# Channel attention folded into a squared-ReLU feed-forward: early weight forms kept in SBUF per batch, late ones loaded singly, sums of squares moved to transfers, rounding of v in the third groups

## The chip, the core and the metric

The program runs on one core of a Trainium2 chip. The metric is the time of one execution on the device in microseconds (us). The kernel before takes 2139.14 us (median of three runs, 2138.82 to 2139.2). Times inside the program come from one profiled execution.

## The reference: what is computed

q, k and v are four batches of 6080 rows and 256 columns, in float32. Each column of q and k is divided by its norm over the 6080 rows; a 256 x 256 matrix of products of k's columns with q's columns is taken over the rows; a softmax over it gives `a`; the rows of v are multiplied by `a` and then go through a feed-forward with 2048 hidden columns.

```python
def _attn_ref(q, k, v, tau):
    qn = q / (np.linalg.norm(q, axis=1, keepdims=True) + 1e-06)
    kn = k / (np.linalg.norm(k, axis=1, keepdims=True) + 1e-06)
    s = kn.transpose(0, 2, 1) @ qn / tau
    s = s - s.max(-1, keepdims=True)
    a = np.exp(s)
    a /= a.sum(-1, keepdims=True) + 1e-09
    return (v @ a).astype(np.float32)

def _moe_ref(x, w_in, w_out):          # x: the 4 x 6080 rows of v @ a
    h = np.maximum(x @ w_in, 0.0)      # w_in 256 x 2048
    return (h * h @ w_out).astype(np.float32)
```

## The kernel before

**The computation as it is arranged.** `a` is multiplied into w_in first: W = a @ w_in (256 x 2048) is made once per batch, and the feed-forward then reads v itself. Float32 precision comes from splitting each operand of a matmul into a high and a low part (`_hi`, `_lo`) and adding three products. A rounding of this kind is two instructions: a cast on ScalarE (ACT) that makes the high part, and a subtraction on VectorE (DVE) that makes the low part.

**Blocks, groups, periods.** In the text the batches are counted 1 to 4; names of tiles carry 0 to 3. The rows of v come in 12 blocks per batch (ten of 512, two of 480). The first two blocks of batch 1 and the last of batch 4 are done plainly. The 45 others are done in four groups of 512 hidden columns each; one group of one block is a period, and the 180 periods are counted by `k` (k = 40, 88 and 136 are the first of batches 2, 3 and 4). A period makes the hidden values by a scheme of seven products of the Strassen kind, in place of eight: seven combinations of quarters of W (the forms A11, S1, S2, A12, S4, S3 and A22) meet seven combinations of quarters of the block of v. TensorE's order in `period(k)` is A11 (into `ps_b`), S1 (`ps_h`), a window of output matmuls of earlier groups, S2 (`ps_c`), A12 (`ps_b`), S4 (`ps_h`), S3 (`ps_c`), matmuls of the attention, another output window, A22 (`ps_c`), another output window. Between them ScalarE and VectorE form sums, ReLU, squares and roundings of the hidden values.

**The attention of the next batch** runs beside these periods: `attention(b)` is a generator that is moved on at fixed points of each period (`side("dve")`, `side("sq")`, `side("pe")`, `side("act")`, `side("mid")`). It takes q and k in 25 chunks, one per period: load, rounding (ACT, DVE), squares (ACT, in place), the product into `gram`, and the addition of the squares into `acc`. After the last chunk come the norms, the softmax, W and the forms of W; these are rounded, stored to DRAM scratch by `keep_blocks` and `keep_sums`, and read back by the periods of the next batch. I call the stretch in which this happens, at the end of each of batches 1 to 3, the forming stretch.

**Forms in the kernel before.** `load_forms(k, late)` brings each period's forms in four transfers: the early forms A11, S1, S2 (two of 384 KB, high and low) and the late ones A12, A22, S3, S4 (two of 512 KB). They lie in the tags `w_hi` and `w_lo` with buffers for two periods; the early ones of period k+2 are asked for after S2 of period k, the late ones of period k+1 after S1 of period k.

**What sets the order.** Each engine runs its instructions in the order in which the program gives them. For SyncE (SP), which issues most loads, the loads of forms and the first chunks of q and k are placed in its queue by the framework's scheduler; the stores of forms and the later chunks stay at their place in the program. An issue whose condition is not met holds back all that stands behind it in SP's queue; the same is true of GpSimd (POOL), which issues the loads of v, the accumulation of partial outputs in DRAM order (`o<-o`), and the outputs.

**v.** `parts_of_v` loads the next block, forms its seven combinations and rounds them in two pieces of 1024 and 768 columns. `v_step` moves it at six points of a block: `V_STEPS` for batches 1 to 3 (both pieces done in the second and third group), `V_LAST` for batch 4 (in the third and fourth).

## Time and profile before

| | us |
|---|---|
| median of three runs | 2139.14 |
| span of the profiled execution | 2137.0 |
| the runs' median less that span | 2.14 |
| TensorE (PE) busy | 2123.9 |
| VectorE busy | 1947.1 |
| ScalarE busy | 1818.6 |
| GpSimd busy | 403.4 |

The profile shows one execution. Its own time is given only as its span, from the first to the last instruction; the runs' median stands 2.14 us above it. The page gives busy time by engine, the chain of work that ended last, and the costliest groups; views of the trace give waits, timelines, and busy time by stretch. A matmul is pipelined with the next, so a busy TensorE is one without a visible hole, not one at its peak. "<-" between tiles means "written from"; "<-" before an engine or a transfer names who ended a wait. All operations are recorded at line 27, the helper that issues them in program order, save the loads that the scheduler places.

### The profile page before, as it was taken

The numbers are of one execution on the slowest core, as the hardware profiler recorded it, in microseconds if no ns is written. First come the engines' busy times: TensorE is split into PE (matmuls) and PEld (weight loads), VectorE is DVE, ScalarE is ACT, GpSimd is POOL, SyncE is SP. The second block draws the span as 40 slices with busy tenths as digits, with TensorE's granted clock in tenths as the row PEclk, the third lists the DMA queues.
The fourth block names the chain that finished last, engine by engine and source line by source line (L and its number), as shares of the span: only waits on it lengthen the run. The fifth ranks groups of instructions, "written<-read, shape, count | busy, mean of one in ns | idle before, by whom it ended". The sixth has DMA issues, their size and how long they took to land.

```text
span 2137.0 us, 43905 instructions
## 1 busy us (share of the span) xinstructions
PE 2123.9 (99%) x16990; PEld 2066.1 (97%) x16990; DVE 1947.1 (91%) x2577; ACT 1818.6 (85%) x2708; POOL 403.4 (19%) x506
## 2 busy tenths in 40 slices
PE   9999999999999999999999999999999999999999
PEld 8789999999999999999999999999999999999998
DVE  6898999998999999988999999999899999999993
ACT  5887888888888888878888888878888999999995
POOL 0000121211222121221222121121212122122121
PEclk9999999999999999999999999999999999999999
DMA  9777888889998888788999788887999788788783
GB/s 345 234 232 264 240 255 252 235 239 283 303 297 262 251 251 262 234 241 247 292 303 288 248 255 257 249 234 229 325 322 314 233 241 252 220 247 248 233 256 86
DMA packets 258865, 548.24 MB, mean 257 GB/s; under 512 B 26848, under 2 KB 120672, under 8 KB 258656
## 3 DMA queue, kind: packets, MB, share of 16 engines
q1 hardware_dynamic: 193696, 449.32, 62.3%
q0 software_dynamic: 64960, 96.11, 20.9%
q8 instruction: 134, 2.20, 0.4%
q14 instruction: 75, 0.61, 0.1%
HBM read 431.75 MB, written 64.23 MB: 232 GB/s over the span
## 4 chain that ended last, share of the span: by engine, by line
PE 89%; DVE 6%; ACT 2%; DMA 2%; issue 1%; SPq 0%; DVEq 0%; ACTq 0%
PE ps_o L27 41%; PE ps_c L27 16%; PE ps_h L27 14%; PE ps_b L27 11%; PE gram L27 4%; DVE x L27 2%; PE ps_w L27 2%; PE ps_o_m L27 1%; ACT x L27 1%; DMA wf<-wf_kept 1%; DVE s_lo L27 1%; DVE acc L27 1%; DMA qk<-in_k 1%; DVE A_lo L27 0%; DMA qk<-in_q 0%
## 5 line engine op out<-in xcount | busy, mean ns | idle before, releaser
L27 DVE TENSOR_TENSOR s_lo<-x,s_hi 128x1024 fp32r<-128x1024 f32 (+1 forms) x384 | 464.0, 1208 | 44.4 <-ACT s_hi L27 44.1
L27 PE MATMUL ps_c<-v_hi,wf 128*128 128x256 f32 (+1 forms) x2160 | 466.9, 280 | 4.4 <-DVE x L27 2.2
L27 POOL DMA_DIRECT2D o<-o x225 | 245.4, 1253 | 1102.7 <-ACT o L27 689.7
L27 ACT CAST s_hi<-x 128x1024 fp32r<-128x1024 f32 (+1 forms) x384 | 399.7, 1041 | 37.6 <-DVE x L27 27.9
L27 DVE TENSOR_TENSOR x<-x 128x1024 f32<-128x1024 f32 (+3 forms) x540 | 389.6, 722 | 10.3
L27 PEld LDWEIGHTS ps_c<-v_hi,wf 128*128 128x128 f32 x2160 | 367.4, 188 | 7.8 <-ACT ps_c L27 3.3
L27 ACT ACTIVATE x<-x 128x512 f32<-128x512 f32 (+2 forms) x540 | 350.0, 648 | 21.7 <-DVE x L27 9.2
L27 PE MATMUL ps_b<-v_hi,wf 128*128 128x256 f32 (+1 forms) x1440 | 309.7, 279 | 1.8 <-DVE nx L27 1.1
L27 PE MATMUL ps_h<-v_hi,wf 128*128 128x256 f32 (+1 forms) x1440 | 309.1, 278 | 0.0
L27 PE MATMUL ps_c<-v_lo,wf 128*128 128x256 f32 (+1 forms) x1080 | 300.9, 279 | 0.0
L27 DVE TENSOR_TENSOR A_lo<-x,A_hi 128x1024 fp32r<-128x1024 f32 (+3 forms) x360 | 276.9, 792 | 18.8 <-ACT A_hi L27 15.3
L27 ACT CAST A_hi<-x 128x1024 fp32r<-128x1024 f32 (+3 forms) x360 | 254.4, 707 | 38.4 <-DVE x L27 25.5
L27 PEld LDWEIGHTS ps_b<-v_hi,wf 128*128 128x128 f32 x1440 | 245.2, 188 | 2.3 <-DVE nx L27 1.3
L27 PEld LDWEIGHTS ps_h<-v_hi,wf 128*128 128x128 f32 x1440 | 244.9, 188 | 0.0
L27 ACT COPY x<-ps_c 128x512 f32<-128x512 f32 (+1 forms) x180 | 105.1, 584 | 158.3 <-PE ps_c L27 158.0
L27 PEld LDWEIGHTS ps_c<-v_lo,wf 128*128 128x128 f32 x1080 | 203.2, 188 | 0.1
L27 PE MATMUL ps_b<-v_lo,wf 128*128 128x256 f32 (+1 forms) x720 | 200.6, 279 | 0.0
L27 PE MATMUL ps_h<-v_lo,wf 128*128 128x256 f32 (+1 forms) x720 | 200.4, 278 | 0.0
L27 DVE TENSOR_TENSOR x<-x,ps_h 128x512 f32<-128x512 f32 (+1 forms) x180 | 122.4, 680 | 76.9 <-PE ps_h L27 76.6
L27 PE MATMUL ps_o<-s_hi,wo_hi 128*128 128x256 f32 (+3 forms) x954 | 190.1, 295 | 0.5 <-ACT s_hi L27 0.5
L27 PE MATMUL ps_o<-s_hi,wo_lo 128*128 128x256 f32 (+3 forms) x954 | 190.2, 295 | 0.0
L27 PE MATMUL ps_o<-s_lo,wo_hi 128*128 128x256 f32 (+3 forms) x954 | 190.0, 295 | 0.1
(166 smaller groups left out, 5166.9 us busy)
## 6 DMA issues: line engine op xcount, KB each, us to landing
wf<-wf_kept SPq DMA_DIRECT2D x360, 512.0 KB, 5.3
wf<-wf_kept SPq DMA_DIRECT2D x360, 384.0 KB, 4.9
o<-o POOLq DMA_DIRECT2D x114, 256.0 KB, 5.9
qk<-in_k SPq DMA_DIRECT2D x87, 256.0 KB, 4.3
qk<-in_q SPq DMA_DIRECT2D x87, 256.0 KB, 4.8
v<-in_vT POOLq DMA_DIRECT2D x76, 256.0 KB, 5.1
out_T<-o POOLq DMA_DIRECT2D x152, 128.0 KB, 4.7
o<-o POOLq DMA_DIRECT2D x76, 128.0 KB, 6.2
```

The costliest lines, as they stand in the source:

```text
L27: return lambda *args, **kwargs: self.tc.keep_in_program_order(issue(*args, **kwargs))
```

## The change

It has three parts.

1. **Forms.** The early forms of a batch and group (768 KB, high and low together) get a buffer of their own for each of the four groups (`w_own0` to `w_own3`, 6 KB per partition) and are loaded once per batch by `load_early`; the other periods of the batch use what is there. The late forms come singly, 256 KB each (high and low of one form), through a ring of four buffers of 2 KB per partition (`w_ring`): `load_late(k + 1, form)` stands right behind the product of period k that used the same form. The scratch in DRAM is cut to match (`wf_early`, `wf_later`), so a part of the form sums is stored in three transfers instead of two. SBUF for forms stays 32 KB per partition. W itself (batch 1, and the last block) uses pieces of the same buffers, and the first chunks of q and k use `w_own` and four tags of the hidden values as landing space.
2. **Squares.** For the attentions of batches 3 and 4 (which run beside batches 2 and 3), the 24 additions on VectorE per batch become accumulating transfers issued by GpSimd, as it already was for five chunks of batch 2. The chunk loaded next is one earlier than before, and the softmax begins one period later, so the forms of batch 3 are stored one period later and those of batch 4 two.
3. **Roundings of v.** `V_LAST` holds for all batches: the pieces of 1024 and 768 columns are rounded in the third group and at the start of the fourth.

```diff
@@ Gram.add_squares
-                if self.b == 1 and c < HEAD:
+                if self.b > 1 or self.b == 1 and c < HEAD:
                     pool_engine.dma_start(a, sq, accum_op=ALU.add)
@@ attention(b)
         def add_and_load(c):
             g.add_squares(c)
+            c -= b > 1
             if c0 <= c and c + ahead < g.n:
                 load(c + ahead)
...
         yield from until("mid")
         add_and_load(g.n - 1)
         yield
+        if b > 1:
+            yield from until("mid")
+            yield
         yield from until("dve")
         yield from softmax_and_W(b)
@@ keep_sums
-        early, later = wf_kept[b, g, i]
         src = part.bitcast(F32).rearrange("p (r s m) -> p r s m", r=2, s=4)
-        issue(early[:, :, 1:3, :], src[:, :, 0:2, :])
-        issue(later[:, :, 2:4, :], src[:, :, 2:4, :])
+        issue(wf_early[b, g][:, i, :, 1:3, :], src[:, :, 0:2, :])
+        for s, form in ((2, S3), (3, S4)):
+            issue(wf_later[b, g, form[0]][:, i], src[:, :, s, :])
@@ forms of a period
-    def load_forms(k, late):
-        if k < len(groups):
-            b, _, j = groups[k]
-            for i in range(2):
-                n = (3, 4)[late]
-                t = WF[k, late, i] = wpool.tile([P, 2, n, P], F32R, tag=("w_hi", "w_lo")[late], name=f"wf{k}_{late}_{i}")
-                nc.sync.dma_start(t.bitcast(F32), wf_kept[b, j, i][late])
...
+    def load_early(k):
+        if k >= len(groups):
+            return
+        b, n, j = groups[k]
+        if k >= GPB and groups[k - GPB][0] == b:
+            WF[k, 0] = WF[k - GPB, 0]
+            return
+        own = own_tile(j, 3 * 2 * 2 * P, F32R, f"wf{k}_own")
+        WF[k, 0] = own.rearrange("p (i r s m) -> p i r s m", i=2, r=2, s=3)
+        nc.sync.dma_start(WF[k, 0].bitcast(F32), wf_early[b, j])
+
+    def load_late(k, form):
+        if k < len(groups):
+            b, n, j = groups[k]
+            f = form[0]
+            t = ring_tile([P, 2, 2, P], f"wf{k}_{f}")
+            WF[k, f] = t.rearrange("p i r (s m) -> p i r s m", s=1)
+            nc.sync.dma_start(t.bitcast(F32), wf_later[b, j, f])
+        elif form in (A12, S4):
+            load_plain((A12, S4).index(form))
@@ v_step
+    V_LAST_FROM = 0
-        steps = V_LAST if b == B - 1 else V_STEPS
+        steps = V_LAST if b >= V_LAST_FROM else V_STEPS
@@ period(k)
         product(k, H, S1, T1, start=True)
-        load_forms(k + 1, 1)
...
-        load_forms(k + 2, 0)
+        load_early(k + 2)
...
         product(k, B2, A12, B21)
+        load_late(k + 1, A12)
...
         product(k, H, S4, B22)
+        load_late(k + 1, S4)
...
         product(k, C, S3, T3)
+        load_late(k + 1, S3)
...
         product(k, C, A22, T4)
+        load_late(k + 1, A22)
```

**SP's queue inside batch 3.** The rows are the loads of forms of periods 92 and 93 (`wf<period>_<piece>`; 128x768 is 384 KB, 128x1024 is 512 KB, 128x512 is 256 KB) and the chunks of q and k (`qk3_..`). Before:

```order
L983 DMA wf92_1_0_14723<-wf_kept2_0_0_4_154 128x1024
L983 DMA wf92_1_1_14725<-wf_kept2_0_1_4_156 128x1024
L420 DMA qk3_4_14670<-in_k 128x512
L421 DMA qk3_4_14670<-in_q 128x512
L983 DMA wf93_0_0_14759<-wf_kept2_1_0_3_157 128x768
L983 DMA wf93_0_1_14761<-wf_kept2_1_1_3_159 128x768
L983 DMA wf93_1_0_14876<-wf_kept2_1_0_4_158 128x1024
L420 DMA qk3_5_14835<-in_k 128x512
L421 DMA qk3_5_14835<-in_q 128x512
L983 DMA wf93_1_1_14878<-wf_kept2_1_1_4_160 128x1024
```

After:

```order
L1013 DMA wf92_3_14825<-wf_later2_0_3_171 128x512
L1013 DMA wf92_4_14883<-wf_later2_0_4_172 128x512
L435 DMA qk3_4_15021<-in_k 128x512
L436 DMA qk3_4_15021<-in_q 128x512
L1013 DMA wf93_1_14947<-wf_later2_1_1_173 128x512
L1013 DMA wf93_2_14959<-wf_later2_1_2_174 128x512
L1013 DMA wf93_3_14969<-wf_later2_1_3_175 128x512
L435 DMA qk3_5_15160<-in_k 128x512
L1013 DMA wf93_4_15031<-wf_later2_1_4_176 128x512
L436 DMA qk3_5_15160<-in_q 128x512
```

A period has four loads of late forms in place of four of both kinds; none of early forms is left inside a batch.

**SP's queue at the passage from batch 2 to batch 3.** The rows are the stores of the form sums of the last group (`wS_hi2_3`, `wS_lo2_3`) and the loads around them; k = 88 is the first period of batch 3. Before:

```order
L420 DMA qk3_1_14224<-in_k 128x512
L983 DMA wf88_1_0_14143<-wf_kept2_0_0_4_154 128x1024
L983 DMA wf88_1_1_14145<-wf_kept2_0_1_4_156 128x1024
L27 DMA wf_kept2_3_0_3_165<-wS_hi2_3_14076 256x1x256
L27 DMA wf_kept2_3_0_4_166<-wS_hi2_3_14076 256x1x256
L27 DMA wf_kept2_3_1_3_167<-wS_lo2_3_14077 256x1x256
L27 DMA wf_kept2_3_1_4_168<-wS_lo2_3_14077 256x1x256
L421 DMA qk3_1_14224<-in_q 128x512
L983 DMA wf89_0_0_14182<-wf_kept2_1_0_3_157 128x768
L983 DMA wf89_0_1_14184<-wf_kept2_1_1_3_159 128x768
L983 DMA wf89_1_0_14289<-wf_kept2_1_0_4_158 128x1024
L983 DMA wf89_1_1_14291<-wf_kept2_1_1_4_160 128x1024
```

After:

```order
L1013 DMA wf88_4_14300<-wf_later2_0_4_172 128x512
L27 DMA wf_early2_3_132<-wS_hi2_3_14268 128x2x256
L27 DMA wf_later2_3_3_183<-wS_hi2_3_14268 128x2x128
L27 DMA wf_later2_3_2_182<-wS_hi2_3_14268 128x2x128
L27 DMA wf_early2_3_132<-wS_lo2_3_14269 128x2x256
L27 DMA wf_later2_3_3_183<-wS_lo2_3_14269 128x2x128
L27 DMA wf_later2_3_2_182<-wS_lo2_3_14269 128x2x128
L1004 DMA wf91_own_14505<-wf_early2_3_132 128x1536
L1013 DMA wf89_1_14371<-wf_later2_1_1_173 128x512
L1013 DMA wf89_2_14383<-wf_later2_1_2_174 128x512
L1013 DMA wf89_3_14393<-wf_later2_1_3_175 128x512
L1013 DMA wf89_4_14445<-wf_later2_1_4_176 128x512
```

Before, the stores stand in front of loads of other groups' forms. After, the load of the last group's early forms (`wf91_own`), which reads what the stores write, stands in front of the late forms of period 89; the same is so for `wf43_own` and the late forms of period 42, and for `wf139_own` and those of period 136.

**VectorE in the third and fourth group of a block of batch 2** (periods 50 and 51). `v_lo1_3` is the low part of v's next block, `acc2` the sum of squares, `x50` and `x51` the hidden values, `ps_h`/`ps_c` TensorE's results. Before:

```order
L27 TENSOR_TENSOR acc2_7752<-acc2_7752,qk2_7_8402 128x1024
L27 TENSOR_TENSOR v_lo1_3_8676<-v1_3_8241,v_hi1_3_8675 128x768
L27 TENSOR_TENSOR A_lo_50_8839<-x50_8747,A_hi_50_8838 128x2x512
L27 TENSOR_TENSOR A_lo_50_8839<-x50_8747,A_hi_50_8838 128x2x256
L27 TENSOR_TENSOR x50_8747<-x50_8747 128x2x2x256
L27 TENSOR_TENSOR qk_lo2_8_8826<-qk2_8_8550,qk_hi2_8_8825 128x2x512
L27 TENSOR_TENSOR x50_8747<-x50_8747 128x512
L27 TENSOR_TENSOR x51_8899<-x51_8899,ps_h51_8888 128x512
L27 TENSOR_TENSOR x50_8747<-x50_8747 128x512
L27 TENSOR_TENSOR x51_8899<-x51_8899,ps_c51_8886 128x512
L27 TENSOR_TENSOR s1_lo_50_8942<-x50_8747,s1_hi_50_8941 128x1024
```

After:

```order
L27 TENSOR_TENSOR v_lo1_3_8792<-v1_3_8342,v_hi1_3_8791 128x1024
L27 TENSOR_TENSOR A_lo_50_8881<-x50_8784,A_hi_50_8880 128x2x512
L27 TENSOR_TENSOR A_lo_50_8881<-x50_8784,A_hi_50_8880 128x2x256
L27 TENSOR_TENSOR x50_8784<-x50_8784 128x2x2x256
L27 TENSOR_TENSOR qk_lo2_8_8868<-qk2_8_8732,qk_hi2_8_8867 128x2x512
L27 TENSOR_TENSOR x50_8784<-x50_8784 128x512
L27 TENSOR_TENSOR v_lo1_3_8792<-v1_3_8342,v_hi1_3_8791 128x768
L27 TENSOR_TENSOR x51_8936<-x51_8936,ps_h51_8929 128x512
L27 TENSOR_TENSOR x50_8784<-x50_8784 128x512
L27 TENSOR_TENSOR x51_8936<-x51_8936,ps_c51_8927 128x512
L27 TENSOR_TENSOR s1_lo_50_8981<-x50_8784,s1_hi_50_8980 128x1024
```

The addition into `acc2` is gone, the piece of 1024 columns now stands where it and the piece of 768 stood, and the piece of 768 stands in front of the first sum of the fourth group.

## Rows read from the trace of the kernel before

**Rows 1.** The page: the span, its part 1 (busy time, share of the span and number of instructions of each engine) and its part 4 (shares of the chain of work that ended last, by engine).

```profile
span 2137.0 us, 43905 instructions
...
PE 2123.9 (99%) x16990; PEld 2066.1 (97%) x16990; DVE 1947.1 (91%) x2577; ACT 1818.6 (85%) x2708; POOL 403.4 (19%) x506
...
PE 89%; DVE 6%; ACT 2%; DMA 2%; issue 1%; SPq 0%; DVEq 0%; ACTq 0%
```

**Rows 2.** Busy time by stretch. Columns: the stretch and its length, then busy us and (in brackets) the number of instructions of PE, PEld, DVE, ACT and POOL, the granted clock, the share of the DMA engines that was busy, GB/s.

```profile
150.00:400.00 250.00, 247.73 (x2012) 242.15 (x2011) 237.17 (x322) 212.82 (x315) 38.05 (x48) 1.00 0.80 248
400.00:640.00 240.00, 238.21 (x1966) 233.15 (x1965) 221.09 (x327) 198.82 (x311) 50.83 (x62) 1.00 0.90 275
640.00:900.00 260.00, 260.00 (x2196) 258.56 (x2195) 248.36 (x309) 229.49 (x334) 50.98 (x63) 1.00 0.83 251
900.00:1140.00 240.00, 238.10 (x1973) 233.67 (x1973) 218.32 (x314) 197.82 (x308) 50.42 (x63) 1.00 0.90 277
1140.00:1400.00 260.00, 260.00 (x2192) 258.42 (x2192) 248.34 (x305) 229.69 (x332) 52.77 (x64) 1.00 0.84 252
1400.00:1650.00 250.00, 249.28 (x2063) 244.75 (x2062) 227.05 (x327) 205.96 (x321) 52.52 (x64) 1.00 0.92 287
```

**Rows 3.** The same view and columns for the second group of one block of batch 2, from one A12 product to the next.

```profile
656.90:668.46 11.56, 11.56 (x99) 11.43 (x97) 11.53 (x15) 10.32 (x15) 2.19 (x2) 1.00 0.90 259
```

**Rows 4.** The timeline of VectorE around the passage from the third to the fourth group of a block of batch 2, and in the last line TensorE's first matmul of the A22 product of that fourth group. Columns: start and duration in us, engine, line, operation, tiles, shapes, count, and in brackets idle time before it and who ended it.

```profile
720.32 1.22 DVE L27 TENSOR_TENSOR acc<-acc,qk 128x1024 f32<-128x1024 f32 x1
...
721.45 0.95 DVE L27 TENSOR_TENSOR v_lo<-v,v_hi 128x768 fp32r<-128x768 f32 x1
...
727.24 0.69 DVE L27 TENSOR_TENSOR x<-x,ps_h 128x512 f32<-128x512 f32 x1 [0.23 <-PE ps_h L27]
...
728.45 0.68 DVE L27 TENSOR_TENSOR x<-x,ps_c 128x512 f32<-128x512 f32 x1
...
731.19 0.28 PE L27 MATMUL ps_c<-v_hi,wf 128*128 128x256 f32 x1
```

**Rows 5.** The same place in batch 4: the last sum of VectorE before A22, TensorE's last matmul of the output window, and its first of A22.

```profile
1727.85 0.68 DVE L27 TENSOR_TENSOR x<-x,ps_c 128x512 f32<-128x512 f32 x1
...
1728.39 0.28 PE L27 MATMUL ps_o<-A_lo,wo_hi 128*128 128x256 f32 x1
...
1728.59 0.39 PE L27 MATMUL ps_c<-v_hi,wf 128*128 128x256 f32 x1
```

**Rows 6.** What TensorE waited for: tile and line of the waiting matmuls, the releaser, then us in total, times, longest.

```profile
PE ps_c L27 <- DVE x L27: 2.2, 5, 0.9
...
PE ps_c L27 <- ACT ps_c L27: 2.1, 3, 0.9
...
PE ps_b L27 <- DVE nx L27: 1.1, 1, 1.1
...
PE ps_b L27 <- DMA wf<-wf_kept: 0.7, 1, 0.7
```

**Rows 7.** ScalarE's timeline in the third group of the second such block of batch 1, and TensorE's matmul that waits for it.

```profile
223.44 1.08 ACT L27 CAST v_hi<-v 128x1024 fp32r<-128x1024 f32 x1
...
226.53 0.58 ACT L27 COPY ps_c<-ps_b 128x512 f32<-128x512 f32 x1
...
227.17 0.38 PE L27 MATMUL ps_c<-v_hi,wf 128*128 128x256 f32 x1 [0.66 <-ACT ps_c L27]
```

**Rows 8.** VectorE's additions of squares (count, ns min/median/max, first and last start, forms), then from part 6 of the page the issues of transfers: queue, count, KB each, median us from issue to landing.

```profile
L27 DVE TENSOR_TENSOR acc<-acc,qk x67: 677/1218/1222, 201.1 to 1419.2; 128x1024 f32<-128x1024 f32 x61, 128x512 f32<-128x512 f32 x3, 64x512 f32<-64x512 f32 x3
...
wf<-wf_kept SPq DMA_DIRECT2D x360, 512.0 KB, 5.3
...
wf<-wf_kept SPq DMA_DIRECT2D x360, 384.0 KB, 4.9
...
qk<-in_q SPq DMA_DIRECT2D x87, 256.0 KB, 4.8
```

**Rows 9.** Time from issue to landing of transfers in a stretch: first the loads of forms between 640 and 900 us, then the loads of forms between 900 and 1140 us, then the two stores of the low parts of form sums (wS_lo) between 615 and 619 us, then the two between 1119 and 1124.2 us.

```profile
DMA to landing us min/median/max: 2.9/4.9/8.1
DMA to landing us min/median/max: 2.9/5.4/11.6
DMA to landing us min/median/max: 7.5/8.2/8.8
DMA to landing us min/median/max: 9.2/9.8/10.4
```

**Rows 10.** The two passages from batch 1 to 2 and from batch 2 to 3, in the order of time: VectorE makes the low part of the last group's form sums (612.21 and 1116.40); TensorE's first matmul of an A12 product (the lines into ps_b at 624.29, 1120.15, 1129.67 and 1140.29); and the one matmul of the whole program that waits for a load of forms (1136.96).

```profile
612.21 1.22 DVE L27 TENSOR_TENSOR wS_lo<-w_sums,wS_hi 128x1024 fp32r<-128x1024 f32 x1
...
624.29 0.28 PE L27 MATMUL ps_b<-v_hi,wf 128*128 128x256 f32 x1
...
1116.40 1.22 DVE L27 TENSOR_TENSOR wS_lo<-w_sums,wS_hi 128x1024 fp32r<-128x1024 f32 x1
...
1120.15 0.28 PE L27 MATMUL ps_b<-v_hi,wf 128*128 128x240 f32 x1
...
1129.67 0.28 PE L27 MATMUL ps_b<-v_hi,wf 128*128 128x256 f32 x1
...
1136.96 0.50 PE L27 MATMUL ps_b<-v_hi,wf 128*128 128x256 f32 x2 [0.73 <-DMA wf<-wf_kept]
...
1140.29 0.28 PE L27 MATMUL ps_b<-v_hi,wf 128*128 128x256 f32 x1
```

More of the change, by code (lines that the diff above doesn't have):

```diff
@@ L163 @@
     wi_kept = [[scratch.tile([P, NC, GRP], F32, name=f"wi_kept{g}_{i}") for i in range(2)] for g in range(NG)]
-    wf_kept = {
-        (b, g, i): [scratch.tile([P, 2, n, P], F32, name=f"wf_kept{b}_{g}_{i}_{n}") for n in (3, 4)]
+    wf_early = {(b, g): scratch.tile([P, 2, 2, 3, P], F32, name=f"wf_early{b}_{g}") for b in range(B) for g in range(NG)}
+    wf_later = {
+        (b, g, f): scratch.tile([P, 2, 2, P], F32, name=f"wf_later{b}_{g}_{f}")
         for b in range(B)
         for g in range(NG)
-        for i in range(2)
+        for f in range(1, 5)
     }
@@ L195, in keep_blocks @@
     def keep_blocks(b, g, i, part, issue):
-        early, later = wf_kept[b, g, i]
-        src = part.bitcast(F32).rearrange("p c (r i m) -> p c r i m", r=2, i=2)
-        for to, c, f in ((early[:, :, 0, :], 0, 0), (later[:, :, 0, :], 1, 0), (later[:, :, 1, :], 1, 1)):
-            issue(to, src[:, c, :, f, :])
+        src = lambda c, f: part(c).bitcast(F32).rearrange("p (r i m) -> p r i m", r=2, i=2)[:, :, f, :]
+        issue(wf_early[b, g][:, i, :, 0, :], src(0, 0))
+        issue(wf_later[b, g, A12[0]][:, i], src(1, 0))
+        issue(wf_later[b, g, A22[0]][:, i], src(1, 1))
     def keep_sums(b, g, i, part, issue):
-        early, later = wf_kept[b, g, i]
         src = part.bitcast(F32).rearrange("p (r s m) -> p r s m", r=2, s=4)
-        issue(early[:, :, 1:3, :], src[:, :, 0:2, :])
-        issue(later[:, :, 2:4, :], src[:, :, 2:4, :])
+        issue(wf_early[b, g][:, i, :, 1:3, :], src[:, :, 0:2, :])
+        for s, form in ((2, S3), (3, S4)):
+            issue(wf_later[b, g, form[0]][:, i], src[:, :, s, :])
+    by_half = lambda tile: lambda c: tile[:, c, :]
+    A11, S1, S2 = ((0, at) for at in range(3))
+    A12, S4, S3, A22 = ((1 + at, 0) for at in range(4))
     wp_kept = [[scratch.tile([P, NC, GRP], F32, name=f"wp_kept{g}_{i}") for i in range(2)] for g in range(NG)]
@@ L325, in forms_of_W @@
         w32, S = room()
-        vector.tensor_add(w32, w_hi.bitcast(F32), w_lo.bitcast(F32))
+        for c in range(NC):
+            vector.tensor_add(w32[:, c, :], w_hi(c).bitcast(F32), w_lo(c).bitcast(F32))
         yield
@@ L329, in forms_of_W @@
             keep_blocks(b, g, i, part, nc.sync.dma_start)
-        if b == B - 1:
-            for kept, part in zip(wp_kept[g], (w_hi, w_lo)):
-                nc.sync.dma_start(kept, part.bitcast(F32))
         w4, S4 = v(w32), S.rearrange("p (r s m) -> p r s m", r=2, s=4)
@@ L392, with ring_tile, own_tile, W_tiles @@
     OWN_BUFS = {"qk": QK_BUFS, "dec": 1}
-    FAST_TAGS = ("qk",) * QK_BUFS + ("w_lo",) * NG + ("w_hi",) * NG
+    FAST_TAGS = ("qk",) * QK_BUFS + tuple(f"w_own{g}" for g in range(NG)) + ("s1_hi", "s1_lo", "s2_hi", "s2_lo")
+    def ring_tile(shape, name):
+        return wpool.tile(shape, F32R, tag="w_ring", name=name, bufs=4)
+    def own_tile(g, cols, dt, name):
+        return wpool.tile([P, 6, C], dt, tag=f"w_own{g}", name=name, bufs=1).rearrange("p a c -> p (a c)")[:, 0:cols]
+    def W_tiles(b, g):
+        own, more = own_tile(g, 3 * GRP, F32R, f"w{b}_{g}"), ring_tile([P, GRP], f"w_lo{b}_{g}")
+        return (lambda c: own[:, c * GRP : (c + 1) * GRP]), (lambda c: more if c else own[:, 2 * GRP : 3 * GRP])
     class Gram:
@@ L999, in two_halves @@
         return ps_h.tile([P, 2, T // 2], F32, tag=tag, name=name)
-    A11, S1, S2 = ((0, at) for at in range(3))
-    A12, A22, S3, S4 = ((1, at) for at in range(4))
     T3, B21, B22, B11, T1, T2, T4 = range(7)
@@ L1013, in product @@
         for p in range(2):
-            late, at = form
-            w_hi, w_lo = (WF[k, late, i][:, p, at, :] for i in range(2))
+            piece, at = form
+            w_hi, w_lo = (WF[k, piece][:, i, p, at, :] for i in range(2))
             for i, (wt, vt) in enumerate(((w_hi, v_hi), (w_hi, v_lo), (w_lo, v_hi))):
@@ L1420 @@
         if i == 26:
-            load_forms(0, 0)
-            load_forms(0, 1)
+            load_early(0)
+            for form in (A12, S4, S3, A22):
+                load_late(0, form)
     for _ in prep:
@@ L1441 @@
     vprep = [parts_for(OLD + 1)]
-    load_forms(1, 0)
+    load_early(1)
     def left_over(*products):
```

37 lines of the change are left out of this document (18 added, 19 removed).

## The prediction

> **What bounds the kernel now.** I read the page first. TensorE is busy for 2123.9 us of a span of 2137.0 and has 89% of the chain that ended last; VectorE is busy for 91% [rows 1]. So the time is TensorE's work plus the holes in it, and the change leaves that work as it is (its matmuls are the same in number and shape). I therefore asked where the holes lie. The view by stretch [rows 2] gives, as length less TensorE's busy time, 250 - 247.73 = 2.27 us from 150 to 400, 1.79 to 640, 0 to 900, 1.90 to 1140, 0 to 1400 and 0.72 to 1650: 6.68 us in all. That is the most which the removal of waits can bring there in this view. The steady parts of batches 2 and 3, from 640 to 900 and from 1140 to 1400, have no hole at all, though VectorE is nearly full there: 11.53 of 11.56 us in one group [rows 3]. The clock granted to TensorE is 1.00 in all these rows, so it is no part of the argument. The list of TensorE's waits says what the holes are: 2.2 us for VectorE's sums and 2.1 us for ScalarE's copies in front of products into `ps_c`, 1.1 us for a norm, and a single wait of 0.7 us for a load of forms [rows 6].
>
> **Forms, inside a batch.** A period asked for 2 x 384 + 2 x 512 = 1792 KB [rows 8] and now asks for 1024 KB. TensorE does not wait for transfers in these stretches, so the saving gives no time by itself. The cost could be lead: a late form is asked for one period before its use, some 11.5 us less its own product [rows 3], and loads of forms land in 4.9 us, at worst 8.1 [rows 9]. That leaves over 2 us. In the forming stretches the worst landing is 11.6 us against periods of 9.5 (1129.67 - 1120.15) to 10.6 (1140.29 - 1129.67) [rows 9, 10], so a few could come 1 to 2 us late; but the traffic that made them slow falls by the 768 KB per period. Bounds: 0 to one such wait of 1.6 us in each of three stretches, 4.8. I take 0, the median's answer. The one wait for a form, 0.7 us [rows 6], at 1136.96 in the first matmuls of period 89 [rows 10], was for an early form; these now stand well ahead in SP's queue. It goes: -0.7.
>
> **Forms, at the passage between batches.** This is where I see a new wait. The load of the last group's early forms reads what the last stores write, and it is placed in SP's queue in front of the late forms that TensorE needs next (the second pair of orders above). Queued behind it are all four late forms of that period, and TensorE waits for them in order. I work it out for two of the three passages.
> Batch 1 to 2: VectorE ends the low sums at 612.21 + 1.22 = 613.43 [rows 10]; their store lands 7.5 us after its issue [rows 9], at 620.9; then the own load goes out and the first late form right behind it. A load of 256 KB lands in 4.8 us [rows 8], at 625.7. Its A12 product starts at 624.29 [rows 10]: 1.4 us late.
> Batch 2 to 3: the sums come one period later than in the trace, 1116.40 + 1.22 + 9.52 = 1127.14; the store takes 9.2 [rows 9], to 1136.3, the late form 4.8, to 1141.1; the product is due at 1140.29 less the 0.7 that went, 1139.6 [rows 10]: 1.5 late.
> Batch 3 to 4 I have no such rows for; with less traffic beside it, as nothing is left to attend to, I take 1.0. Together +3.9 us.
> Bounds: with the quickest load, 2.9 us, both come in time (623.8 and 1139.2): 0; nothing below 0, since TensorE has no other wait there. With the slowest of rows 9 (8.8 + 8.1, and 10.4 + 11.6) they are 6.0 and 9.5 late, and with 9.5 for the third, 25.
> Two rules of the Trainium skill bear on these steps. The page "DMA: Bandwidth & Descriptors", section "Bandwidth", advises transfers of at least 1 MiB and gives 0.95 us for 64 KB and 6.15 us for 1 MB; that speaks against single forms, yet an estimate on a straight line between its figures is 2.0 us for 256 KB, by which both late forms would be in time and the sum 3.9 us lower. The row of 4.8 us was taken beside this kernel's own traffic, and I keep it. The same page, section "Queues, rings and completion order", says that a transfer's completion mark lands only after all earlier writes of the same DMA engine. The stores' 7.5 to 10.4 us here fit that; by it the first passage, with several loads now ahead of the stores, would rather have 9.2 us and be 3.1 us late, and the sum 1.7 higher.
>
> **Squares.** 48 additions of 1.22 us [rows 8], 58 us of VectorE, go. They lie where TensorE has no hole [rows 2], so they bring 0. What they add: a chunk's load waits for a transfer of 512 KB to land, some 5.3 us [rows 8], with a period of 11 us between the issue of the one and the turn of the other. Behind that load on SP stand late forms, behind the accumulation on GpSimd stand the partial outputs. Bounds: 0, and, where GpSimd is held up in front of it, one wait as long as the form's 0.7 us [rows 6] in each of 12 blocks, 8.4. I take 0. The later softmax moves the norm's wait of 1.1 us [rows 6] to another group; I leave it as it is.
>
> **Roundings of v.** In batches 2 and 3 the piece of 1024 columns takes the place of the addition into `acc` (1.22 us for 1.22), and the piece of 768 (0.95 us) is moved behind a few sums. VectorE reaches its last sum before A22 at the same time as before. That sum ends at 728.45 + 0.68 = 729.13 and A22 starts at 731.19: 2.06 us to spare [rows 4]. In batch 1, where the addition stays, 1.22 - 0.23 of idle time is added, 0.99 us, still inside 2.06. So 0. The other bound is batch 4, which has these roundings already: the sum ends at 1728.53, A22 starts at 1728.59, 0.20 us after the last output matmul, where matmuls follow at 260 / 2196 = 0.12 [rows 2], and takes 0.39 in place of 0.28 [rows 5]. That is 0.19 us a block, over 10 + 12 + 12 blocks 6.5 us. I take 0, the row of the same batch. On ScalarE the cast of 1.08 us at 223.44 leaves the second group; the copy behind it was 0.66 us late for TensorE [rows 7]. That goes: -0.7. Two other waits of this kind (the rest of the 2.1 us) and those for VectorE's sums [rows 6] I leave standing, half gone and half moved being as likely; together they are the 3.6 us that could still go.
>
> **The sum.** 2137.0 - 0.7 - 0.7 + 3.9 = 2139.5 us of span; the runs' median stands 2.14 above the span, so 2141.6 us, 0.1% above 2139.14. A change within 0.2% (2134.9 to 2143.4) I call none, as a measurement of this kernel can hardly tell it.
>
> **Rivals.**
> In time: the late forms at the passages land soon enough. 2137.0 - 1.4 + 2.1 = 2137.7. For it: the quick end of the landings, and lighter traffic from the middle of each batch. Against it: the passages' own traffic, since a batch's first block still loads everything.
> Passages far late: the stores report late and the loads behind them wait together; past some 11 us (first) or 12.5 us (second) for store and load together each further us is lost, three times. At 5 us each 2137.0 - 1.4 + 15 + 2.1 = 2152.7. For it: 9.2 and 11.6 us in rows 9.
> The third group as in batch 4: A22 waits for VectorE in 34 blocks, 2141.6 + 6.5 = 2148.1. For it: VectorE is nearly full [rows 3]. Against it: the 2.06 us.
> Chunks late by the accumulations: with the passages in time 2137.7 + 8.4 = 2146.1.
> Faster: the passages in time and the waits of the forming stretches gone with a lighter VectorE, all 6.7 us: 2137.0 - 6.7 + 2.1 = 2132.4. For it: the holes lie just where attention, forms and roundings meet. Against it: most follow from norms and sums that stay.
> That the change does nothing is excluded by the orders above: one own load per batch and group, one late form at a time.
>
> **How the numbers follow.** Passages a little late, 0.36 (2138 to 2145); in time, 0.24 (2134.5 to 2140); far late, 0.14; the third group, 0.07; late chunks, 0.05; faster, 0.14. The first is the likeliest, and its value is the forecast. Slower by over 0.2%: 0.14 + 0.07 + 0.05 and 0.08 of the first, 0.34. Faster: 0.13 of the last and 0.02 of the second, 0.15. Within: 0.51. The range leaves out about half of the far late case and two thirds of the faster one: 2133.5 to 2150.
>
> **What would show it.** In TensorE's waits: the wait of 0.7 us for a form in period 89 gone, and in its place waits into `ps_b` for a load of a late form at some 623 to 627, 1138 to 1143 and near 1655 us, of 1 to 2 us each; in SP's timeline a gap before each `own` load at these places that ends with a store's landing. From 640 to 900 and 1140 to 1400 TensorE should stay without holes, with some 29 us less of VectorE in each batch. Waits into `ps_c` for VectorE once per block in batches 1 to 3 would prove the third rival, waits of `gram` for q or k the fourth, and no wait for forms at the passages would prove the central term wrong.

## The result, and the profile after

The change makes the kernel slower: 2159.93 us (median of four runs, 2157.06 to 2160.43) against 2138.98, a ratio of 1.0097 [1.0083, 1.0112]. The forecast was 2141.6 with a range up to 2150; it missed by 18 us.

The page of the kernel after shows: span, busy times, shares of the chain that ended last, and issues of transfers (queue, count, KB each, median us from issue to landing).

```profile
span 2158.0 us, 44502 instructions
...
PE 2131.8 (99%) x16990; PEld 2069.9 (96%) x16990; DVE 1899.0 (88%) x2533; ACT 1820.2 (84%) x2708; POOL 441.1 (20%) x554
...
PE 80%; DVE 10%; ACT 5%; DMA 3%; issue 2%; SPq 1%; DVEq 0%; ACTq 0%
...
wf<-wf_later SPq DMA_DIRECT2D x720, 256.0 KB, 3.5
...
acc<-qk POOLq DMA_DIRECT2D x46, 512.0 KB, 7.5
```

Against [rows 1] VectorE is busy for 48 us less (the 58 us of the prediction are the additions' durations, and those of neighbours overlap a little: in [rows 4] 720.32 + 1.22 reaches past 721.45), and TensorE the same 16990 matmuls; but the chain now runs 10% through VectorE (6% before) and 5% through ScalarE (2%). The stretches of [rows 2] in the kernel after (same columns):

```profile
150.00:400.00 250.00, 245.83 (x1989) 239.61 (x1989) 234.13 (x319) 210.10 (x311) 37.52 (x48) 1.00 0.65 182
400.00:640.00 240.00, 234.81 (x1929) 229.17 (x1928) 215.63 (x322) 195.39 (x305) 49.74 (x61) 1.00 0.75 212
640.00:900.00 260.00, 258.94 (x2173) 256.58 (x2173) 226.31 (x287) 227.73 (x329) 66.86 (x85) 1.00 0.86 222
900.00:1140.00 240.00, 237.61 (x1960) 232.85 (x1959) 212.84 (x305) 195.99 (x306) 52.72 (x65) 1.00 0.77 208
1140.00:1400.00 260.00, 257.09 (x2142) 254.44 (x2142) 221.37 (x284) 224.21 (x326) 66.47 (x82) 0.99 0.86 224
1400.00:1650.00 250.00, 247.65 (x2040) 242.92 (x2039) 222.68 (x315) 206.08 (x317) 54.39 (x69) 1.00 0.78 218
```

The same stretch of time now holds fewer matmuls everywhere (1989 for 2012 in the first, 2173 for 2196 in the third). The holes grew from 6.68 us to 18.07 in all, and those of 640 to 900 and 1140 to 1400, which had none, are 1.06 and 2.91 us. A busy row hides the rest: a matmul that is held up for a few tenths of a microsecond counts partly as busy. TensorE's waits (tile and line, releaser, us in total, times, longest) answer to [rows 6]:

```profile
PE ps_c L27 <- ACT ps_c L27: 6.0, 9, 1.6
PE ps_c L27 <- DVE x L27: 4.6, 7, 1.3
PE ps_c L27 <- DMA wf<-wf_later: 3.0, 3, 1.8
PE ps_b L27 <- DMA wf<-wf_later: 2.7, 2, 2.4
PE ps_b L27 <- DVE nx L27: 1.4, 2, 1.1
```

Waits for ScalarE's copies went from 2.1 to 6.0 us, for VectorE's sums from 2.2 to 4.6, and 5.7 us of waits for late forms are new. Since waits alone don't reach 21 us, I compared when the first matmul of each block's first A12 product starts. The shift grows nearly everywhere:

| k | before | after | shift |
|---|---|---|---|
| 0 | 163.36 | 162.42 | -0.9 |
| 40 (batch 2 begins) | 603.78 | 608.51 | 4.7 |
| 68 | 918.03 | 927.46 | 9.4 |
| 88 (batch 3 begins) | 1129.67 | 1141.89 | 12.2 |
| 112 | 1402.36 | 1417.99 | 15.6 |
| 140 | 1694.90 | 1715.19 | 20.3 |

From one such product to the next, only the last period of a block is longer in steady stretches: 11.21 us before; after, 11.97 in batch 1 and 11.43 in batches 2 and 3.

### The profile page after: what moved, and what is told of

The parts are those of the page before. It is cut to its first block, busy times and chain, and to the rows that moved or that the text cites. A ratio compares the mean times of both kernels' runs of the same rounds, so it can differ in the third digit from the quotient of the medians.

```text
span 2158.0 us, 44502 instructions
## 1 busy us (share of the span) xinstructions
PE 2131.8 (99%) x16990; PEld 2069.9 (96%) x16990; DVE 1899.0 (88%) x2533; ACT 1820.2 (84%) x2708; POOL 441.1 (20%) x554
## 4 chain that ended last, share of the span: by engine, by line
PE 80%; DVE 10%; ACT 5%; DMA 3%; issue 2%; SPq 1%; DVEq 0%; ACTq 0%
PE ps_o L27 36%; PE ps_c L27 15%; PE ps_h L27 12%; PE ps_b L27 10%; PE gram L27 4%; DVE x L27 3%; ACT x L27 2%; PE ps_w L27 2%; DVE s_lo L27 1%; DMA wf<-wf_later 1%; DVE v_lo L27 1%; PE ps_o_m L27 1%; DVE acc L27 1%; DVE A_lo L27 1%; ACT s_hi L27 1%
## 5 line engine op out<-in xcount | busy, mean ns | idle before, releaser
L27 PE MATMUL ps_c<-v_hi,wf 128*128 128x256 f32 (+1 forms) x1440 | 312.3, 280 | 7.7 <-DVE x L27 4.6
L27 PEld LDWEIGHTS ps_c<-v_hi,wf 128*128 128x128 f32 x1440 | 245.6, 189 | 11.0 <-DVE x L27 6.2
L27 PE MATMUL ps_c<-v_lo,wf 128*128 128x256 f32 (+1 forms) x720 | 201.0, 279 | 0.0
L27 DVE SCALAR_TENSOR_TENSOR x<-x 128x1024 f32<-128x1024 f32 (+3 forms) x180 | 176.2, 979 | 0.0
L27 PE MATMUL ps_c<-v_hi,wf_own 128*128 128x256 f32 (+1 forms) x720 | 158.3, 283 | 6.1 <-ACT ps_c L27 6.0
L27 PE MATMUL ps_b<-v_hi,wf 128*128 128x256 f32 (+1 forms) x720 | 155.0, 279 | 2.7 <-DMA wf<-wf_later 2.7
L27 PE MATMUL ps_b<-v_hi,wf_own 128*128 128x256 f32 (+1 forms) x720 | 155.1, 279 | 1.4 <-DVE nx L27 1.4
L27 PE MATMUL ps_h<-v_hi,wf 128*128 128x256 f32 (+1 forms) x720 | 155.7, 280 | 0.0
L27 PE MATMUL ps_h<-v_hi,wf_own 128*128 128x256 f32 (+1 forms) x720 | 154.6, 278 | 0.0
L27 PEld LDWEIGHTS ps_o<-s_lo,wo_hi 128*128 128x128 f32 x954 | 146.2, 188 | 6.2 <-DVE s_lo L27 0.5
```

Of the source, the lines that this page charges most:

```text
L27: return lambda *args, **kwargs: self.tc.keep_in_program_order(issue(*args, **kwargs))
```

## The experiments

In the expectations, A holds that the roundings of v carry most of the loss, B that the forms do; R holds that a late form is asked for too short a time before its use; C, P and Q are explained where they come up.

### The three parts one by one

Each part alone, on the kernel before (squares alone, roundings alone) or by undoing the others in the kernel after (forms alone):

```diff
 v_only (kernel before)
-        steps = V_LAST if b == B - 1 else V_STEPS
+        steps = V_LAST
 squares_only (kernel before; with the two edits of attention)
-                if self.b == 1 and c < HEAD:
+                if self.b > 1 or self.b == 1 and c < HEAD:
 forms_only (kernel after; the squares undone in all three places)
-    V_LAST_FROM = 0
+    V_LAST_FROM = 3
```

v_only: 

> The kernel before with the new roundings of v alone. Theory A (the moved piece of 768 columns stands on VectorE in front of the first sum of the fourth group; ScalarE's ReLU waits for that sum, comes 0.9 us late, and its copy into ps_c then holds TensorE up at S2 of the next block): 0.6 to 0.8 us in each of 34 blocks, 20 to 27 us, so about 2159 to 2166 us, since the additions of squares stay in all batches. Theory B (the loss of the changed kernel comes from the transfers of forms and from their later stores): no change, 2139 us within 2. The prediction's rival (A22 waits for VectorE): 6.5 us, with waits at A22 instead of S2.

forms_only: 

> The changed kernel with the other two parts undone: early forms kept, late ones through the ring. Theory A: only the waits for transfers remain, about 3 us at the passages between batches and up to 3 us at other late forms, so 2142 to 2145 us. Theory B: most of the 21 us, 2155 us or more. If the ring were harmless: 2138 to 2139 us.

squares_only: 

> The kernel before with the sums of squares of batches 3 and 4 done by accumulating transfers, and their softmax one period later. Theory A: about 0 (VectorE is relieved where TensorE had no hole), 2137 to 2140 us. Theory B: the forms come one and two periods later and meet other groups, +3 to +6 us, 2142 to 2145 us.

Then each part left out: no_v is the kernel after with `V_LAST_FROM = 3`, no_squares the kernel after with the squares undone, no_forms the kernel before with squares and roundings.

no_v: 

> The changed kernel with the old points of v's rounding in batches 1 to 3. Theory A: batch 1 gains back 4 us and batches 2 and 3 some 0.2 us a block and part of the waits around softmax and forms, 8 to 11 us: 2149 to 2152 us. Theory B: unchanged, 2158 to 2161 us.

no_squares: 

> The changed kernel with the additions of squares back on VectorE and the softmax at its old time. Theory A: in batches 2 and 3 the piece of 768 columns is no longer paid for by a removed addition, so the loss per block rises from 0.2 to about 0.75 us, +12 us over 22 blocks, less what the earlier forms give back at the passages: 2165 to 2173 us. Theory B (late stores are the loss): 2150 us or less.

no_forms: 

> The changed kernel with the old transfers of forms (both other parts kept). Theory A: the waits for late forms go, 6 us less than the changed kernel: 2152 to 2156 us. Theory B: 2140 to 2145 us.

| kernel | median us | ratio to before | us over before |
|---|---|---|---|
| v_only | 2169.55 | 1.0145 [1.0128, 1.0162] | 31 |
| forms_only | 2150.58 | 1.0054 [1.0039, 1.0069] | 12 |
| squares_only | 2176.66 | 1.0173 [1.0145, 1.0201] | 39 |
| no_v (forms and squares) | 2145.51 | 1.0033 [1.0021, 1.0045] | 7 |
| no_squares (forms and v) | 2166.87 | 1.0134 [1.0117, 1.0151] | 28 |
| no_forms (squares and v) | 2219.30 | 1.0379 [1.0364, 1.0395] | 81 |

Every part alone costs time. The largest share of the change's 21 us is the roundings': without them 7 us are left, so 14 go with them. B's price for the forms was too high and A's too low. Of the six expectations only no_squares' was met; v_only came out above A's range and no_v below it. The squares came out far from what any theory gave: 39 us alone (2167 to 2182 us in four runs), yet -7 us when added to forms and roundings (28 to 21) and -5 when added to the forms (12 to 7). No sum of three prices describes these; the next sections look for the mechanisms.

### The roundings of v: which instruction pays

VectorE and ScalarE in the fourth group of a block of batch 1 in the kernel before, and ScalarE's copy at the start of the next block (columns as in [rows 4]):

```profile
288.82 0.69 DVE L27 TENSOR_TENSOR x<-x,ps_h 128x512 f32<-128x512 f32 x1 [0.23 <-PE ps_h L27]
...
289.54 1.30 ACT L27 ACTIVATE x<-x 128x512 f32<-128x512 f32 x2
...
296.87 0.58 ACT L27 COPY ps_c<-ps_b 128x512 f32<-128x512 f32 x1
```

The same place in the kernel after, and TensorE's first matmul of S2 in the next block:

```profile
289.11 0.95 DVE L27 TENSOR_TENSOR v_lo<-v,v_hi 128x768 fp32r<-128x768 f32 x1
289.98 0.69 DVE L27 TENSOR_TENSOR x<-x,ps_h 128x512 f32<-128x512 f32 x1
...
290.69 1.30 ACT L27 ACTIVATE x<-x 128x512 f32<-128x512 f32 x2 [0.92 <-DVE x L27]
...
298.01 0.58 ACT L27 COPY ps_c<-ps_b 128x512 f32<-128x512 f32 x1
...
298.64 0.38 PE L27 MATMUL ps_c<-v_hi,wf_own 128*128 128x256 f32 x1 [0.48 <-ACT ps_c L27]
```

Before, VectorE had waited 0.23 us for TensorE and ended the first sum just in time for ScalarE's ReLU. After, the piece of 0.95 us stands in front of that sum; ScalarE stands idle for 0.92 us. Behind the ReLU ScalarE has no gap up to its copy into `ps_c`, so the delay reaches S2 of the next block 8 us later. A22 of the same block, which I had watched, does not wait. In five other blocks it does (k = 3, 27, 71, 87 and 135, the first block and some of the forming stretches), 3.5 us in all for VectorE's sums, where the kernel before has no such wait and no_v one of 0.35; the longest:

```profile
964.82 0.39 PE L27 MATMUL ps_c<-v_hi,wf 128*128 128x256 f32 x1 [1.28 <-DVE x L27]
```

What the last periods of the blocks gained or lost can be summed: over batches 1 to 3, the 34 periods with k mod 4 = 3 take 12.3 us more in the kernel after than in no_v (5.6, 4.5 and 2.2 by batch), where the two profiled spans differ by 11.8. In v_only, where the addition into `acc` stays on VectorE, they take 11.97 in the steady blocks of batches 2 and 3 as well, and the loss is 31 us.

The next run moves the piece of 768 columns, and with it the next load of v, one point later, behind the sums. C holds that this only moves the loss.

```diff
-    V_LAST = ..., (2, "mid"), (3, "dve")
+    V_LAST = ..., (2, "mid"), (3, "act")
```

> The changed kernel with one rounding moved: the piece of 768 columns (and the next load of v) stands on VectorE behind the two sums of the fourth group instead of in front of them. Nothing is added or left out. Theory A (ScalarE's ReLU waits for these sums, and TensorE at S2 for ScalarE): most of the 14 us that the rounding costs come back, 2146 to 2150 us, and the waits into ps_c for ScalarE's copy fall from 6.0 to about 2.5 us. Theory C (the place does not matter, VectorE's and ScalarE's time in the third and fourth group does): 2157 to 2161 us with the same waits.

Measured: 2157.69 us, 1.0092 [1.0077, 1.0107], 2 us less than the change, with intervals that overlap. TensorE's waits in it:

```profile
PE ps_h L27 <- DVE v_lo L27: 4.9, 6, 2.3
PE ps_b L27 <- DMA wf<-wf_later: 4.4, 3, 3.8
```

The waits into `ps_c` for ScalarE fall from 6.0 us to a single one of 0.3, and the steady last periods are back at 11.21 us, which shows the mechanism. ScalarE's casts of v stand where the change put them, so they aren't what the steady blocks paid for. But S1 of the next block now waits for v itself in six blocks (4.9 us, the longest 2.26 at 202.12), batch 4, which uses the same steps, pays 0.17 us a block (9.99 to 10.16), and late forms wait 4.4 us in place of 2.7. C was right in the sum, A in the cause. These amounts don't add up to all of the 12 us that remain above no_v; the rest is not split.

### The passages between batches

SyncE's queue and TensorE at the passage from batch 2 to 3 in the kernel after:

```profile
1142.29 0.61 SPq L27 DMA_DIRECT2D wf_early<-wS_lo  x1
...
1148.60 0.33 SPq L1004 DMA_DIRECT2D wf_own<-wf_early  x1
1149.03 11.21 SPq L1013 DMA_DIRECT2D wf<-wf_later  x8
...
1154.08 0.38 PE L27 MATMUL ps_b<-v_hi,wf 128*128 128x256 f32 x1 [2.38 <-DMA wf<-wf_later]
```

The own load goes out 6.3 us after the store, the late forms right behind it, and A12 waits 2.38 us: the predicted wait, at the predicted place. In forms_only, where this passage comes one period earlier, it costs 5.29 us. From batch 1 to 2, in the same views of the same kernel, there are two waits:

```profile
618.18 0.33 SPq L435 DMA_DIRECT2D qk<-in_k  x1
...
619.10 0.36 SPq L1013 DMA_DIRECT2D wf<-wf_later  x1
...
623.20 0.35 PE L27 MATMUL ps_c<-v_hi,wf 128*128 128x256 f32 x1 [1.75 <-DMA wf<-wf_later]
...
625.22 0.33 SPq L1004 DMA_DIRECT2D wf_own<-wf_early  x1
...
630.80 0.38 PE L27 MATMUL ps_b<-v_hi,wf 128*128 128x256 f32 x1 [0.32 <-DMA wf<-wf_later]
```

The smaller (0.32) is the one predicted. The larger (1.75) is A22's form: it stands in SP's queue behind a load of q and k that lands in a buffer still held by the form sums. Before, the same A22 waited 0.42 us, for VectorE.

P: the own load's place in front of the late forms is the cause, and issuing it last in the period, in the program's order, cures it. Tried on forms_only, on no_v, and on the change together with the edit of v_behind_sums (both_fixed):

```diff
-        load_early(k + 2)
         late_step()
...
         load_late(k + 1, A22)
+        load_early(k + 2)
...
-        nc.sync.dma_start(WF[k, 0].bitcast(F32), wf_early[b, j])
+        sync.dma_start(WF[k, 0].bitcast(F32), wf_early[b, j])
...
-            nc.sync.dma_start(t.bitcast(F32), wf_later[b, j, f])
+            sync.dma_start(t.bitcast(F32), wf_later[b, j, f])
```

forms_own_last: 

> The forms alone (2150.6 us with the scheduler's order) with the loads of forms in program order and the load of early forms behind the period's four late ones. Theory P (the loss of the forms is the load that waits for stores in front of the late forms at the passages): 2139 to 2143 us, the waits of 5.9 us into ps_b for late forms gone. Theory R (a lead of one period and pieces of 256 KB are too little): 2147 us or more, with waits for late forms all through the forming stretches.

no_v_own_last: 

> Forms and squares without the roundings (2145.5 us), with the same order of loads as in forms_own_last. Theory P: 2 to 4 us less, 2141 to 2144 us. Theory R: 2145 us or more.

both_fixed: 

> The whole change with both edits (loads of early forms last, the piece of 768 behind the sums). Theories A and P together: 2159.9 less 10 to 14 less 2 to 4, 2143 to 2147 us; slower than that if the two costs overlap.

Measured: 2153.39 us (1.007 [1.0055, 1.0085]), 2151.94 (1.0062 [1.0045, 1.0079]) and 2160.43 (1.0102 [1.0087, 1.0117]): none faster than its base. P falls as put. In forms_own_last A22 of the first passage waits longer than before:

```profile
625.13 0.35 PE L27 MATMUL ps_c<-v_hi,wf 128*128 128x256 f32 x1 [4.61 <-DVE v_lo L27]
```

Its form went out at 617.87, still behind the load of q and k (616.95), and landed at 625.00. The view names the low part of v, which ended just then but is the next block's; in no_v_own_last it names the form for the same wait (4.07 us). Another 3.7 us are lost to own loads that now come late themselves. In these three runs, whatever stands first on SP, something behind it is late.

Q: it is the blocked issue in a shared queue. Take both kinds of waiting loads (the own loads of batches 2 to 4, and the first three chunks of q and k for the attentions of batches 3 and 4) out of SP's queue, onto GpSimd's:

```diff
-        nc.sync.dma_start(WF[k, 0].bitcast(F32), wf_early[b, j])
+        (nc.sync if b == 0 else pool_engine).dma_start(WF[k, 0].bitcast(F32), wf_early[b, j])
...
-            queue = sync if self.b and c >= HEAD else nc.sync
+            queue = pool_engine if self.b > 1 and c < 3 else sync if self.b and c >= HEAD else nc.sync
```

forms_on_pool: 

> The forms alone (2150.6 us) with the loads that can hold SP's queue up moved to GpSimd's queue: the early forms of batches 2 to 4 and the first three chunks of q and k of batches 3 and 4. The late forms then stand behind nothing but the stores themselves. Theory Q (late forms are held up behind other loads in SP's queue): 2139 to 2143 us and no wait over 1 us for a late form. Theory R (a lead of one period is too short in itself): 2147 us or more, with such waits where SP's timeline shows no gap in front of the load.

no_v_on_pool: 

> Forms and squares (2145.5 us) with the same move. Theory Q: 2140 to 2143 us, the 4.3 us of waits for late forms gone. Theory R: 2145 us or more. If GpSimd is held up by the moved loads, waits for early forms or for v appear instead.

Measured: forms_on_pool 2143.04 us, 1.0017 [1.0008, 1.0026], 8 us better than forms_only. TensorE's waits for late forms in forms_only and, in the last line, in forms_on_pool:

```profile
PE ps_b L27 <- DMA wf<-wf_later: 5.9, 2, 5.3
...
PE ps_c L27 <- DMA wf<-wf_later: 1.7, 1, 1.7
...
PE ps_b L27 <- DMA wf<-wf_later: 0.3, 1, 0.3
```

That bears Q out for the two kinds of loads together and prices the queue at some 8 of the forms' 12 us. Most of the 4 us left is a wait that the move itself made: at 1142.44 S2 waits 3.00 us for ScalarE, which stood idle for 3.88 us until 1138.74 for a chunk of q and k whose loads went out on GpSimd behind an own load. no_v_on_pool stays at 2148.08 (1.0038 [1.0023, 1.0053]), and the 2140 to 2143 us that Q gave are missed: with the accumulating transfers also there, the own loads of batch 4 stand behind outputs on GpSimd, and TensorE waits 4.1 us for own loads, 3.8 of it there.

The last runs build on no_v_on_pool: a fifth buffer in the ring of late forms, by which each is asked for one product earlier; then (best_a) batch 4's own loads back on SP; best_b with batch 4's softmax a period earlier, best_c with two of batch 4's four own loads on GpSimd.

```diff
-        return wpool.tile(shape, F32R, tag="w_ring", name=name, bufs=4)
+        return wpool.tile(shape, F32R, tag="w_ring", name=name, bufs=5)
...
+    AHEAD_LATE = 5
+
+    def load_behind(k, form):
+        at = 4 * k + LATE.index(form) + AHEAD_LATE
+        load_late(at // 4, LATE[at % 4])
...
-        load_late(k + 1, A12)
+        load_behind(k, A12)
...
 best_a: own loads
+        (pool_engine if 0 < b < B - 1 else nc.sync).dma_start(...)
 best_b (best_a and)
-        if b > 1:
+        if b == 2:
 best_c: own loads
+        (pool_engine if 0 < b < B - 1 or b and j > 1 else nc.sync).dma_start(...)
```

no_v_on_pool_ring5: 

> The same with five ring buffers instead of four, so that each late form is asked for one product earlier (A12's some 6 us earlier). Theory Q: as no_v_on_pool within 1 us. Theory R: 2 us or more better than no_v_on_pool.

best_a: 

> Forms and squares without the roundings, five ring buffers, the first three chunks of q and k of batches 3 and 4 and the early forms of batches 2 and 3 on GpSimd's queue, those of batch 4 back on SP's. In no_v_on_pool_ring5 the last own loads were 2.3 to 4 us late at the first period of batch 4, behind outputs on GpSimd; here that wait should go. 2139 to 2142 us, level with the kernel before within 0.2%.

best_b: 

> As best_a, with the softmax of batch 4 one period earlier (one period later than in the kernel before instead of two). The wait of 1.3 us for the norm, which came with the softmax in a first group, should go or change: 1 to 2 us less than best_a, 2137 to 2141 us. If the last accumulations then land too late for the norms, 2 us or more above best_a.

best_c: 

> As best_a, with the early forms of batch 4's third and fourth groups on GpSimd's queue and those of the first two on SP's. In best_a the late forms of period 137 still stood behind the last own load, 2.6 us of waiting. If the queues are the whole loss of forms and squares: 1 to 4 us less than best_a, 2136 to 2139 us, level with the kernel before or just under it. If not: 2139 us or more.

Measured: 2144.42 (1.0024 [1.0015, 1.0034]), 2139.59 (1.0007 [0.9998, 1.0016]), 2140.78 (1.0011 [1.0002, 1.002]) and 2139.24 us (1.0005 [0.9996, 1.0014]). The fifth buffer took 3.7 us off no_v_on_pool, which is R's sign and not Q's, though the intervals of the two ratios overlap; so a longer lead may have a share, which these runs don't separate from the queue's. best_a fell in its range, best_b was no better than best_a, and best_c, though its first period of batch 4 no longer waits for a late form (2.6 us in best_a), came out at the 2139 us or more of its "if not". So with other queues and a fifth buffer forms and squares are level with the kernel before, and none beats it. best_c's row from 640 to 900 us in the view by stretch:

```profile
640.00:900.00 260.00, 260.00 (x2195) 258.56 (x2195) 226.27 (x288) 229.26 (x333) 68.50 (x84) 1.00 0.87 226
```

The traffic of best_c over the whole span, from the page:

```profile
DMA packets 277428, 443.16 MB, mean 207 GB/s; under 512 B 28512, under 2 KB 131296, under 8 KB 277216
```

In this stretch it runs as many matmuls as the kernel before (2195 and 2196) with 22 us less of VectorE; over the program it moves 443 MB for 548. The time doesn't move, since TensorE had no hole there to give up.

### Why the squares cost 39 us alone and no time beside the forms

squares_only from 640 to 900 us in the view by stretch:

```profile
640.00:900.00 260.00, 251.81 (x2087) 249.22 (x2086) 216.46 (x274) 217.49 (x314) 66.45 (x81) 0.99 0.95 277
```

The timeline of squares_only along one chunk's way: the accumulation on GpSimd, the load on SP that waits for it, ScalarE's cast, and TensorE:

```profile
743.60 0.93 POOL L27 DMA_DIRECT2D acc<-qk  x1
...
752.39 0.33 SPq L27 DMA_DIRECT2D qk<-in_k  x1
...
759.29 1.05 ACT L27 CAST qk_hi<-qk 128x1024 fp32r<-128x1024 f32 x1 [3.52 <-DMA qk<-in_q]
...
763.94 0.38 PE L27 MATMUL ps_c<-v_hi,wf 128*128 128x256 f32 x1 [3.15 <-ACT ps_c L27]
```

With the old loads of forms the DMA engines are 0.95 busy (0.83 before [rows 2], 0.87 in no_v). An accumulation then lands in 9.0 us (6.6 in no_v), the chunk's load can go out only after it, ScalarE stands idle 3.52 us for the chunk, and S2 waits 3.15 us for ScalarE's copy queued behind. A second chain runs through SP's queue, as at the passages. The total of TensorE's waits for forms, then one of them:

```profile
PE ps_b L27 <- DMA wf<-wf_kept: 10.7, 10, 2.4
...
840.35 0.93 POOL L27 DMA_DIRECT2D acc<-qk  x1
...
851.22 0.33 SPq L27 DMA_DIRECT2D qk<-in_k  x1
...
852.12 1.80 SPq L987 DMA_DIRECT2D wf<-wf_kept  x4
...
863.02 0.38 PE L27 MATMUL ps_b<-v_hi,wf 128*128 128x256 f32 x1 [2.39 <-DMA wf<-wf_kept]
```

The chunk's load goes out 10.9 us after the accumulation, four loads of forms right behind it, and A12 waits 2.39 us. Waits for forms total 10.7 us, waits for ScalarE's copies 9.4; how many of them go this way, and how the 39 us divide, is not split. The forms' part takes 768 KB per period off the same engines, and the accumulations fit in. With v's roundings added (no_forms, 81 us) the low part of q and k on VectorE is late too: the attention's product into `gram` waits 23.5 us for it, ten times. That this is the same chain, with a VectorE that is asked for more at the wrong time, is argued and not shown.

## Why the prediction was wrong

**The step that failed: "Roundings of v ... So 0".** The working asked whether VectorE would still reach its last sum before A22 in time, with 2.06 us to spare [rows 4]. In the steady blocks it did, and A22 waited in none of them; outside them it waited in five blocks, 3.5 us. But the moved piece stands in front of the first sum of the fourth group, and that sum has another reader, ScalarE's ReLU, which had no slack. The order rows showed the new place; the reader was not looked up. The term was 12 to 14 us (last periods 12.3; no_v against the change 14). The rest of the miss, some 4 us, is that of forms and squares (no_v). The rival "third group as in batch 4" had the right part of the change and, but for those five blocks, the wrong waiter; its 6.5 us came from A22. The -0.7 for the cast at 223.44 [rows 7] came true, as S2 of that period no longer waits, but waits for ScalarE's copies elsewhere brought the total to 6.0 us.

**Passages: the mechanism was right, the parts were off.** Forecast 1.4, 1.5 and 1.0 us, together 3.9; measured 0.32, 2.38 and 0 at the own loads, and 1.75 at A22's form, which I had not seen: the load of q and k in front of it was in the same queue. Waits for late forms total 5.7 us in the change; two S3 forms of the last forming stretch (0.77 and 0.44 us, at 1592.57 and 1625.16) are among them, where the prediction took 0. Stores let the own loads go after 4.1 and 6.3 us, not 7.5 and 9.2; but they went out later than I had placed them, with other issues in front of them in SP's queue (at the second passage at 1142.29, less the shift of 12.2 some 1130, where the working had the sums end at 1127.14). The 4.8 us for the late form were about right: 3.5 is the median of all 720, but at the second passage A12's went out at 1149.03 and its product began at 1154.08, 5.05 us later. The Trainium skill's page "DMA: Bandwidth & Descriptors" (section "Bandwidth") would have given 2.0 us for such a load by the estimate made in the prediction; both measured figures lie above it. The 9.2 us that the prediction drew for the first passage from the same page's rule on completion marks (section "Queues, rings and completion order") are not borne out by the 4.1; the rule itself no run here tests.

**Squares: 0, right only beside the forms.** That the relief of VectorE brings nothing was right with v's roundings at their old place (best_c). With them moved it brings something: without the squares the steady last periods of batches 2 and 3 take 11.97 us (no_squares), with them 11.43. That the accumulations cost nothing held only as the same change lightens the DMA engines: alone they cost 39 us, far beyond the 8.4 of "late chunks". The prediction named the row of 5.3 us for a transfer of 512 KB; it was 6.6 to 9.0 for an accumulation.

**Forms inside a batch.** No hole from forms appeared in the steady stretches (no_v: 260.00 us busy from 640 to 900), and the wait of 0.7 us in period 89 went. Both as predicted.

**What would have been enough.** For forms and squares without the roundings the range would have held no_v's 2145.51, some 4 us above the forecast. What remains of no_v's 7 us beyond 4.6 us of waits for late forms I have not split; part lies before k = 136, where its shift has grown by 2.8 us from k = 112. No run gave v a place in batches 1 to 3 that costs nothing beside `V_STEPS`; the blocks of 480 rows and the forming stretches were not separated from the rest.

## What to carry to other kernels

When an instruction is moved on a full engine, list every reader of what stands behind it at the new place, on all engines, and ask each for its slack; the engine that is made to idle need not be the bottleneck (here ScalarE), and its delay can surface 8 us later. A load that must wait for a store needs a queue in which nothing urgent stands behind it; moving it makes it late for whoever shares the new queue. And time saved on an engine beside a bottleneck without holes buys nothing, while each new dependence can cost.

## What was not expected of the hardware

The accumulating transfers take the DMA engines longer per byte than the loads that they stand beside. forms_only and no_v differ by the squares alone, the kernel before and forms_only by the forms. The queues between 640 and 900 us (packets, MB, share of the 16 engines' time; q1 is SP's, q0 GpSimd's) in the kernel before:

```profile
q1 hardware_dynamic: 19468, 53.13, 61.0%
q0 software_dynamic: 8305, 11.74, 21.3%
```

in forms_only:

```profile
q1 hardware_dynamic: 19456, 35.00, 43.4%
q0 software_dynamic: 8222, 11.66, 22.0%
```

and in no_v:

```profile
q1 hardware_dynamic: 19456, 35.00, 42.4%
q0 software_dynamic: 11134, 22.97, 43.7%
```

The forms took 18.1 MB and 17.6 points off SP's queue (1.0 point per MB) and left GpSimd's as it was; the squares, 22 accumulations of 512 KB, added 11.3 MB and 21.7 points to GpSimd's (1.9 per MB) and left SP's as it was. So from the kernel before to no_v 7 MB less were moved and the engines were no less busy. GpSimd's queue as such is not the reason: of its packets of 4096 bytes in this stretch, the 1280 in forms_only (loads of v and outputs) take 0.16 us in the median; no_v has 2816 more of that size, 128 for each accumulation, and a median of 0.33 us. Whether the adding costs it, or that an accumulation goes from SBUF to SBUF, no run here separates.
